# Batch 0 of a fused attention and FFN kernel: transposing raw queries, using values uncopied, and a new order of the first loads

## Chip, core and metric

The kernel runs on one core of a Trainium2 chip. The metric is device microseconds (us) of one execution, lower is better. The time before is 250.41 us, the median of three runs (249.77 to 251.29). The profile comes from a separate execution of the same program; its times count from the start of that execution's span.

## What is computed

Linear ("cosformer") attention, and a multiplicative feed-forward network on its output. There are 8 batches with 8 heads, 576 positions and 64 features a head. Inputs are fp32; the kernel works in bf16 with fp32 sums.

```python
theta = np.pi / 2.0 * pos / S                      # one angle for each position
phi(x) = concat(relu(x) * cos(theta), relu(x) * sin(theta))   # 64 -> 128 features
q_p, k_p = phi(q), phi(k)
kv  = einsum('bhsf,bhsd->bhfd', k_p, v);  z = sum(k_p, axis=2)
num = einsum('bhsf,bhfd->bhsd', q_p, kv)
den = einsum('bhsf,bhf->bhs', q_p, z) + 1e-06
x   = (num / den)  as 4608 tokens of 512
out = ((x @ w1) * (x @ w2) @ w3) @ w_out           # 512 -> 1024 -> 1024 -> 512
```

Two facts carry the change. The angle belongs to a position, so cos and sin can be multiplied in before a transpose (one number for each partition) or behind it (a row along the free dimension). And relu commutes with the transpose.

## The kernel before

**The plan.** Every instruction's place is written out by hand in the string PLAN. The loop at the end of the kernel (L801) reads it from left to right, and each entry issues its instructions on their engines' queues at once. An engine works its own queue in order; nothing is reordered. An entry `f 0; n 0 4; d 0 4` thus fixes what stands behind what on TensorE, VectorE (DVE), ScalarE (ACT), GpSimd (POOL) and on the DMA queues that POOL and SP issue to. A letter at the end of an entry (V, A, G) is the engine of a copy.

**Chunks.** A batch's 576 positions are five chunks, four of 128 and one of 64 (chunk 4). For each batch, entries load `k`, `q`, `v` (`l`, or `lg` and `lt` behind a gate; `l0` for parts of batch 0). `k b c` and `q b c` make the features of a chunk: the cos half on VectorE (L502), the sin half on ScalarE (L505). `v b c` copies the values to `va`, whose 65th column is 1, so that one matmul gives kv and z (L519). `kv b` (L548; for batch 0 `kv0`, L746) makes kv with 40 matmuls of 65 columns, and copies it to `kvs`. `qt b c` transposes a chunk's query features on TensorE, 8 transposes of 128 columns (L566), and copies them from PSUM to `qpT` (L572). `n b c` is num and den by 8 matmuls of 65 columns into the PSUM tile `pnum`, of which there is one (L580; `n0` has its own, `pfirst`). `d b c` is the division on VectorE: L589, L590, L591. `xt b c` transposes the result on TensorE (L618) and copies it into the FFN's input tile `xT` (L619); `xd b c` does this by a DMA transpose on SP's queue (L611).

**FFN.** There are nine tiles of 512 tokens. Each `f t` issues the next piece of tile t: products with w1 and w2 (L662; for the first two tiles some in quarters of 128 tokens), a copy of the first on ScalarE (L686, L700), their product `abT` on VectorE (L688, L705), and then `abT` times `w34b` (L710) and its copy out.

**The w3 stage.** w3 times w_out is made once: `w34b`. It stands in the plan between tile 0's products and the pieces that use it. `t3 jp` transposes block jp of w3 on VectorE in one instruction into one of three buffers `w3T` (L464), and `w jp lc n` multiplies it by w_out on TensorE (L480); the last is copied by ScalarE (L483).

**The start.** Keys of batch 0 are loaded through SP, everything else through POOL. TensorE runs idle matmuls on zeros (27, then 10, 3 and 3) until there is work. On POOL's queue the order of loads is: v, queries of chunks 0 and 1 (`q02`), v chunk 4, w2 columns 0 and 1, queries 2 and 3 (`q22`), the first part of batch 1's queries, query chunk 4, the second part of batch 1's queries, then the other seven pieces of w1 and w2 with w3 and w_out among and behind them, and then batch 1's keys and values.

Of the kernel before, what the change touches and what calls it, by code (L numbers as in the profile page):

```python
# [10 lines left out]
FP32 = mybir.dt.float32  # L11
BF16 = mybir.dt.bfloat16
I32 = mybir.dt.int32
ALU = mybir.AluOpType
# [21 lines left out]
f 0; xt 0 4 V  # L36
# [24 lines left out]
f 0; n 1 0; xd 1 4; d 1 0  # L61
f 0; q 2 1; v 2 4 G; lt 3 v 0; q 2 0
f 0; n 1 1; d 1 1; k 2 2
f 0; q 2 3
f 0; lg 3 q 1; v 2 1 G; l 3 v 1; q 2 4; k 2 0
f 0; n 1 2; d 1 2
f 0; xt 1 1 V; lt 3 k 0
f 1; k 2 3; xd 1 0; n 1 3; d 1 3; xt 1 2 V
f 1; qd 2 1
f 1; v 2 2 V  # L70
f 1; k 2 4; k 2 1
# [185 lines left out]
f 8  # L257
f 8
f 8; st; st; st; st; st"""
NKP, NVA, NQP, NRQ, NRV, NT3 = 1, 2, 1, 2, 2, 3  # L260


# [14 lines left out]
def _angles(nc, pool):  # L277

    s_i = pool.tile([P, 2 * NCH], I32, name="s_i")
    nc.gpsimd.iota(s_i[0:64, 0:5], pattern=[[1, 5]], base=0, channel_multiplier=5)  # L280
    nc.gpsimd.iota(s_i[64:128, 0:5], pattern=[[1, 5]], base=320, channel_multiplier=4)
    nc.gpsimd.iota(s_i[:, 5:9], pattern=[[1, 4]], base=0, channel_multiplier=4)
    nc.gpsimd.iota(s_i[:, 9:10], pattern=[[1, 1]], base=512, channel_multiplier=1)
    return s_i


def _trig_tables(nc, pool, s_i):

    th = pool.tile([P, 2 * NCH], FP32, name="th")
    nc.vector.tensor_copy(out=th[:], in_=s_i[:])  # L290
    nc.vector.tensor_scalar_mul(out=th[:], in0=th[:], scalar1=math.pi / 2 / S)
    t2 = pool.tile([P, 2 * NCH], FP32, name="t2")
    nc.vector.tensor_mul(out=t2[:], in0=th[:], in1=th[:])

    def poly(outt, coefs):
        nc.vector.tensor_scalar_mul(out=outt[:], in0=t2[:], scalar1=float(coefs[0]))
        for c in coefs[1:-1]:
            nc.vector.scalar_tensor_tensor(out=outt[:], in0=outt[:], scalar=float(c), in1=t2[:],
                                           op0=ALU.add, op1=ALU.mult)

    cosv = pool.tile([P, 2 * NCH], FP32, name="cosv")
    poly(cosv, [-1 / 3628800, 1 / 40320, -1 / 720, 1 / 24, -1 / 2, 1.0])
    nc.vector.tensor_scalar_add(out=cosv[:], in0=cosv[:], scalar1=1.0)
    sinv = pool.tile([P, 2 * NCH], FP32, name="sinv")
    poly(sinv, [-1 / 39916800, 1 / 362880, -1 / 5040, 1 / 120, -1 / 6, 1.0])
    nc.vector.scalar_tensor_tensor(out=sinv[:], in0=sinv[:], scalar=1.0, in1=th[:],
                                   op0=ALU.add, op1=ALU.mult)
    return cosv, sinv


@with_exitstack
def kernel(
# [123 lines left out]
    def clear_rows(i):  # L436

        if i < NVA:
            nc.vector.memset(va_bufs[i][:, :, :, D:D + 1], 1.0)
            nc.vector.memset(va_bufs[i][64:128, 4, :, 0:D], 0.0)  # L440
        for fp in kp_bufs[i:i + 1] + qp_bufs[i:i + 1]:
            nc.vector.memset(fp[64:128, 4, :, :], 0.0)

    clear_rows(0)
# [11 lines left out]
    cosv, sinv = _trig_tables(nc, const, _angles(nc, const))  # L456
    identb = const.tile([P, P], BF16, name="identb")
    make_identity(nc, identb[:])


    def w3_tr(jp):

        w3T = sm.tile([P, 8, 128], BF16, name="w3T", bufs=NT3)
        nc.vector.transpose(out=w3T[:].rearrange("p l (c i) -> p l c i", c=4),  # L464
                            in_=w3b[:, jp, :].rearrange("p (c l j) -> p l c j", c=4, l=8))
        w3Ts[jp] = w3T
# [95 lines left out]
    def q_tr(b, c, on):  # L562
        R = ROWS[c]
        pst = ps_tr.tile([P, 8, 128], BF16, name="pst")
        for h in range(H):
            nc.tensor.transpose(pst[:, h, :], att[b]["qp"][:, c, h, :], identb[:])  # L566
        cols = ds(columns_of(b, c), R)
        if on == "both":
            nc.scalar.copy(out=att[b]["qpT"][:, 0:4, cols], in_=pst[:, 0:4, 0:R])
            nc.vector.tensor_copy(out=att[b]["qpT"][:, 4:8, cols], in_=pst[:, 4:8, 0:R])  # L570
        else:
            on(out=att[b]["qpT"][:, :, cols], in_=pst[:, :, 0:R])  # L572

    def num(b, c, tile=None):
        rows = out_rows(b, c)
# [162 lines left out]

    def kv_first():

        kp, va = att_of(0)["kp"], att_of(0)["va"]
        att[0]["kvs"] = sm.tile([P, H, D + 1], BF16, name="kvs", bufs=2)
        halves = att[0]["halves"] = (kva[:, :], pnum()[:, 0, :])
        for c in range(NCH):
            for h in range(H):
                nc.tensor.matmul(halves[h // 4][:, ds((h % 4) * 65, 65)], lhsT=kp[:, c, h, :],  # L746
                                 rhs=va[:, c, h, 0:D + 1], start=(c == 0 and h % 4 == 0),
                                 stop=(c == NCH - 1 and h % 4 == 3))
# [34 lines left out]
    def gated_store():  # L783
# [6 lines left out]
        "f": lambda t: next(ffn[t]), "w": w34_mm, "w3": load_w3, "wo": load_wout, "w12": w12,  # L790
        "l": load, "lg": gated, "lt": behind_transposes, "l0": load_first_parts, "gx": behind_first_x,
        "k": prep_k, "q": prep_q, "v": prep_v,
        "qc": lambda b, c: prep_q(b, c, sin=False), "qs": lambda b, c, n=H: prep_q(b, c, n, cos=False),
        "kc": lambda b, c: prep_k(b, c, sin=False), "ks": lambda b, c: prep_k(b, c, cos=False),
        "qt": q_tr, "qh": q_tr_halves, "qd": q_dma, "kv": kv, "kv0": kv_first, "kvs0": kvs_first,
# [40 lines left out]
```

## Time and profile before

| what | value |
| --- | --- |
| median of three runs | 250.41 us |
| span of the profiled execution | 249.8 us |
| TensorE weight loads (PEld), busy | 129.8 us, x1855 |
| DMA share by slice, first 28 of 40 slices | 7 to 9 tenths |
| queue q0 (loads and stores by POOL), share of 16 engines | 69.9% |
| last weights of w1 and w2: issued at, us to landing | 20.41, 9.9 |
| first w1 columns: issued at, us to landing | 9.84, 10.3 |
| kv of batch 0 on TensorE | 13.53 to 14.9 |
| kv of batch 1 on TensorE | from 51.67 |

In the lines of a profile, the columns of the timeline are start, duration, engine, source line and operation, the tile written and those read, the shape, how often in a row, and in brackets how long the engine had been idle and what ended that. Matmuls are pipelined: of a group "x4 128x512" with 1.03 us, the next begins 0.86 after its start. A helper's line covers every call of it.

### The profile page before, as it was taken

Reading aid. Unit: us, or ns where it says so; the run is one execution under the profiler, and the core shown is the slowest. Engines: PE = TensorE matmul, PEld = TensorE weight load, DVE = VectorE, ACT = ScalarE, POOL = GpSimd, SP = SyncE. Lnnn points to the kernel's source line nnn. Section 1 sums busy time; section 2 is a strip of 40 time slices with the busy share of each in tenths; the row PEclk is TensorE's granted clock in tenths of the full one; section 3 lists DMA queues with packets and bytes.
Section 4 is the critical chain, followed back from the end, with each engine's and each line's share of the span. In section 5 each row is a group of like instructions: output and inputs, shape, how many; then the busy total and the mean of one; then the engine's idle time right before and its main releaser. Section 6 shows DMA issues by size and latency. Waiting matters only on the chain. (4 is left out here: it accounts for less than half of the span.)

```text
span 249.8 us, 4910 instructions
## 1 busy us (share of the span) xinstructions
PE 241.0 (96%) x1855; PEld 129.8 (52%) x1855; DVE 141.7 (57%) x342; ACT 127.1 (51%) x217; POOL 84.9 (34%) x162
## 2 busy tenths in 40 slices
PE   8978999999999999999999999899999999999994
PEld 2467754455964644445454545355444644444443
DVE  6498667958669546827684370487546506502420
ACT  2698243648567534665477324767643333323332
POOL 7764445425502043107215005307000502569200
PEclk9999999999999999999999999999999999999999
DMA  7999999999997989999999999999676561999513
GB/s 193 184 193 196 200 200 197 198 198 184 151 170 109 166 139 162 160 196 137 153 147 117 189 111 123 140 208 216 154 97 126 139 84 34 219 271 298 192 42 126
DMA packets 87223, 40.69 MB, mean 163 GB/s; under 512 B 51744, under 2 KB 84768, under 8 KB 87200
## 3 DMA queue, kind: packets, MB, share of 16 engines
q0 software_dynamic: 40144, 27.20, 69.9%
q1 hardware_dynamic: 47056, 13.18, 35.5%
q8 instruction: 14, 0.23, 0.4%
q14 instruction: 9, 0.07, 0.1%
HBM read 38.80 MB, written 9.44 MB: 193 GB/s over the span
## 5 line engine op out<-in xcount | busy, mean ns | idle before, releaser
L662 PE MATMUL ffnps<-xT,w2b 128*128 128x512 bf16 (+2 forms) x352 | 76.0, 340 | 1.7 <-ACT osb L716 1.2
L705 DVE TENSOR_TENSOR abT<-asb,ffnps 128x512 bf16<-128x512 bf16 x64 | 43.7, 684 | 59.3 <-PE ffnps L662 57.4
L662 PE MATMUL ffnps<-xT,w1b 128*128 128x512 bf16 (+2 forms) x352 | 76.0, 340 | 0.6 <-DMA xT<-xblk 0.6
L710 PE MATMUL ffnps<-w34b,abT 128*128 128x512 bf16 x280 | 64.5, 379 | 0.0
L700 ACT CAST asb<-ffnps 128x512 bf16<-128x512 f32 x64 | 37.3, 585 | 53.1 <-PE ffnps L662 43.7
L662 PEld LDWEIGHTS <-w2b 128*128 128x128 bf16 x352 | 31.5, 98 | 29.7 <-issue 1.5
L662 PEld LDWEIGHTS <-w1b 128*128 128x128 bf16 x352 | 31.6, 98 | 28.9 <-DMA xT<-xblk 1.1
L710 PEld LDWEIGHTS <-abT 128*128 128x128 bf16 x280 | 26.1, 98 | 28.3
L505 ACT ACTIVATE kp<-kf,sinv 128x512 bf16<-128x512 bf16 (+3 forms) x40 | 28.1, 720 | 9.7 <-DMA kf<-in_k_dram 9.7
L505 ACT ACTIVATE qp<-qs,sinv 128x512 bf16<-128x512 bf16 (+2 forms) x40 | 28.0, 716 | 3.1 <-DMA qs<-in_q_dram 3.1
L591 DVE TENSOR_TENSOR xblk<-pnum,den 128x512 bf16<-128x512 f32 (+1 forms) x39 | 26.9, 691 | 2.0 <-DMA xT<-xblk 0.7
L417 POOL COPY seen<-asb 128x1 bf16<-128x1 bf16 x14 | 2.7, 195 | 68.6 <-ACT asb L700 68.6
L502 DVE TENSOR_SCALAR kp<-kf,cosv 128x512 bf16<-128x512 bf16 (+3 forms) x40 | 15.9, 415 | 9.9 <-DMA kf<-in_k_dram 9.9
L580 PEld LDWEIGHTS <-qpT 128*128 128x128 bf16 x320 | 15.3, 98 | 9.8 <-issue 0.8
L716 ACT COPY early<-ffnps 128x512 f32<-128x512 f32 x19 | 11.1, 582 | 15.5 <-PE ffnps L710 15.4
L580 PE MATMUL pnum<-kvs,qpT 128*128 128x65 bf16 x312 | 16.4, 194 | 1.3 <-DVE xblk L591 0.6
L519 POOL COPY va<-vs 128x512 bf16<-128x512 bf16 (+1 forms) x17 | 10.7, 649 | 18.4 <-PE ffnps L662 9.8
L716 ACT COPY osb<-ffnps 128x512 f32<-128x512 f32 x16 | 9.4, 585 | 14.4 <-PE ffnps L710 14.4
L502 DVE TENSOR_SCALAR qp<-qs,cosv 128x512 bf16<-128x512 bf16 (+1 forms) x40 | 14.8, 389 | 0.9 <-DMA qs<-in_q_dram 0.8
L480 PE MATMUL ffnps<-early,w3T 128*128 128x512 bf16 x64 | 14.3, 379 | 0.1
L453 PE MATMUL unread<-zeros 128*128 128x512 bf16 x43 | 12.2, 451 | 1.2 <-DVE zeros L434 1.2
L650 POOL DMA_DIRECT2D out_dram<-osb x22 | 11.6, 532 | 2.9 <-DMA out_dram<-osb 2.2
(86 smaller groups left out, 187.4 us busy)
## 6 DMA issues: line engine op xcount, KB each, us to landing
out_dram<-osb POOLq DMA_DIRECT2D x10, 256.0 KB, 6.3
qs<-in_q_dram POOLq DMA_DIRECT2D x8, 256.0 KB, 8.2
early<-in_moe_w_dram POOLq DMA_DIRECT2D x8, 256.0 KB, 10.3
qs<-in_q_dram POOLq DMA_DIRECT2D x6, 320.0 KB, 8.4
kf<-in_k_dram POOLq DMA_DIRECT2D x6, 320.0 KB, 9.2
vs<-in_v_dram POOLq DMA_DIRECT2D x6, 320.0 KB, 7.6
kf<-in_k_dram POOLq DMA_DIRECT2D x6, 256.0 KB, 7.1
vs<-in_v_dram POOLq DMA_DIRECT2D x6, 256.0 KB, 8.2
```

The lines of the kernel that those rows point to most:

```text
L453: nc.tensor.matmul(unread[:, :], lhsT=zeros[:, 0:128], rhs=zeros[:], start=True, stop=True)
L480: nc.tensor.matmul(acc[:, :], lhsT=w3T[:, lc, :], rhs=woutb[:, lc, :], start=(lc == 0), stop=(lc == 7))
L502: nc.vector.tensor_scalar(out=dst[:R, c, :, 0:D], in0=src[:R, :, c, :], scalar1=0.0, scalar2=cosv[:R, at:at + 1], op0=ALU.max, op1=ALU.mult)
L505: nc.scalar.activation(out=dst[:R, c, 0:n, D:F], in_=src[:R, 0:n, c, :], func=ACTF.Relu, scale=sinv[:R, at:at + 1], bias=0.0)
L580: nc.tensor.matmul(nt[:, h // 4, ds((h % 4) * 65, 65)], lhsT=qpT[:, h, ds(at, 128)], rhs=kvs[:, h, :], start=True, stop=True)
L591: nc.vector.tensor_tensor(out=xblk[rows], in0=n4[:, :, :, 0:D], in1=den[rows].unsqueeze(3).to_broadcast([R, 2, 4, D]), op=ALU.mult)
L650: on.dma_start(out=rows[:, :, cols], in_=osb[64 * i:64 * i + rows.shape[0], :, cols])
L662: nc.tensor.matmul(out, lhsT=w[:, kc, ts(jc, 128)], rhs=x[:, kc, tok], start=(kc == 0), stop=(kc == 3))
L700: nc.scalar.copy(out=asb[:], in_=aT[:, :])
L705: nc.vector.tensor_mul(out=abT[:, jc, :], in0=asb[:], in1=bT[:, :])
L710: nc.tensor.matmul(ops[:, :], lhsT=abT[:, jc, ts(ms, 128)], rhs=w34b[:, jc, :], start=(jc == 0), stop=(jc == 7))
L716: nc.scalar.copy(out=osb[:, ms % 2, :], in_=ops[:, :])
```

## The change

In batch 0 the queries are no longer turned into features and then transposed. The raw queries of a chunk are transposed twice, into the upper and the lower 64 partitions of a PSUM tile (16 transposes of 64 rows out), and one VectorE instruction takes the maximum with 0, multiplies by a table `waves` and writes `qpT`. The table holds cos in partitions 0 to 63 and sin in 64 to 127, one column a position; it is made once by five fp32 transposes and two copies, in the memory of an output buffer. Batch 0's values are used as they were loaded: kv then takes 64 columns from the values and a 65th column from a second matmul with a column of ones, 80 matmuls in place of 40, with the chunks in the order 4, 0, 2, 3, 1. Rows 64 to 127 of chunk 4 are cleared in the raw values and queries instead of in `va` and `qp`. The transpose of a w3 block may be split in two.

The plan is rewritten from its start to the middle of tile 1 of the FFN; from the second piece of tile 1 on it is the same. Batch 1's queries are loaded behind the first half of w3 and all of w_out, and their features and transposes go into the w3 stage. Two of batch 1's chunks (4 and 0) are transposed into `xT` by TensorE and not by DMA. Of the idle matmuls 27 and 6 are left.

```diff
-l0 q02; k 0 4; k 0 0; idle 10; l0 v4; v 0 0 A; w12 1 0 2; k 0 2; l0 q22; lg 1 q 0; l0 q4; lg 1 q 1; w12 0 0 2; w12 1 4 2; w12 0 2 2; v 0 4 V; v 0 1 V; v 0 2 A; k 0 3; w12 1 6 2; idle 3; w12 1 2 2; q 0 1; w12 0 4 2; w3 3; k 0 1; w3 1; qt 0 1 V; q 0 0 4; w12 0 6 2; wo 1; qc 0 3; v 0 3 A; wo 0; kv0; q 0 2; kvs0 1 A; kvs0 0 A; w3 0; wo 3; w3 2; qh 0 0 V; wo 2; qs 0 3; n 0 1; qt 0 2 A; w3 4; d 0 1; w3 5; qt 0 3 A; q 0 4; n0; w3 6; n 0 2; d 0 0; idle 3; d 0 2; xt 0 1 V; open; w3 7; xt 0 0 A; q 1 2; q 1 0; lg 1 k 0; n 0 3; qt 0 4 V; lg 1 k 1; lg 1 v 0; lt 1 v 1; xt 0 2 A; q 1 3; q 1 1; l 2 k 0
+l0 q02; k 0 4; k 0 0; waves; idle 6; k 0 2; l0 v4; l0 q22; w12 1 0 2; l0 q4; w12 0 0 2; w12 1 2 2; w12 0 2 2; w12 1 4 2; w12 0 4 2; k 0 3; qf 0 0 8; k 0 1 4; w12 1 6 2; w12 0 6 2; w3 3; w3 1; wo 1; wo 0; qf 1 0 8; kv0; kvs0 0 A; kvs0 1 A; w3 0; wo 3; w3 2; wo 2; n0; n 0 1; d 0 0; d 0 1; qf 2 0 8; l 1 q 0; l 1 q 1; w3 4; w3 5; xt 0 0 A; n 0 2; open; xt 0 1 A; w3 6; w3 7
 f 0
-f 0; d 0 3
-f 0; l 2 v 0
-f 0; xt 0 3 V; qt 1 2 V; n 0 4; d 0 4
+f 0; qf 3 0 8; d 0 2; l 1 k 0; l 1 k 1
+f 0; n 0 3; xt 0 2 A; d 0 3; l 1 v 0; l 1 v 1
 f 0
+f 0; xt 0 3 V; qf 4 0 8; l 2 k 0
+f 0; clear 0; l 2 v 0
+f 0; n 0 4; d 0 4
 f 0; clear 1
+f 0; xt 0 4 V
...
-f 0; qt 1 0 V; lg 2 q 0; q 1 4; qt 1 3 A
-f 0; qt 1 1 V
...
-f 0; l 2 k 1; t3 0
 f 0
-f 0; t3 1; qt 1 4 A
-w 0 0 4
-w 0 4 4; l 2 q 1
-w 1 0 4
-w 1 4 4; t3 2; t3 3; t3 4
-w 2 0 4
-w 2 4 4; l 2 v 1; v 1 4 G
-w 3 0 4; v 1 3 G; t3 5; v 1 1 G
-w 3 4 4
-w 4 0 4; k 1 2; l 3 q 0; t3 6
-w 4 4 4; k 1 1; t3 7; k 1 4
-w 5 0 4
-w 5 4 4; k 1 0
-w 6 0 4; v 1 2 V
-w 6 4 4; v 1 0 V; k 1 3
-w 7 0 4; kv 1
-w 7 4 4; v 2 3 G; n 1 4; v 2 0 G
-f 0; d 1 4
-f 0; n 1 0; xd 1 4; d 1 0
+f 0; t3 0 0 4; t3 0 4 4
+w 0 0 4; t3 1; l 2 k 1
+w 0 4 4; q 1 4
+w 1 0 4; t3 2; q 1 0; l 2 q 1
+w 1 4 4
+w 2 0 4; t3 3
+w 2 4 4; qt 1 4 A; q 1 1
+w 3 0 4; l 2 v 1
+w 3 4 4; qt 1 0 V; t3 4; q 1 2; qt 1 1 A
+w 4 0 4
+w 4 4 4; t3 5; q 1 3; v 1 4 G; v 1 3 G; v 1 1 G; l 3 q 0
+w 5 0 4; qt 1 2 V; k 1 2
+w 5 4 4; t3 6; k 1 1
+w 6 0 4; k 1 4; qt 1 3 V
+w 6 4 4; t3 7; k 1 0
+w 7 0 4; v 1 2 V; k 1 3
+w 7 4 4; v 1 0 V; kv 1
+f 0; n 1 4; v 2 3 G; v 2 0 G
+f 0; d 1 4; n 1 0
...
+    oneb = const.tile([P, 1], BF16, name="oneb")
+    nc.vector.memset(oneb[:], 1.0)
+    nc.vector.memset(raw[0, "v"][64:128, :, 4, :], 0.0)
+    nc.vector.memset(raw[0, "q"][64:128, :, 4, :], 0.0)
...
+    for f in range(2):
+        nc.scalar.copy(out=spread[:, :, f, :], in_=trig[:, f, NCH:].unsqueeze(2).to_broadcast([P, NCH, D]))
+
+    def wave_rows():
+        for at, c0, n in ((0, 0, 4), (512, 4, 1)):
+            pst = ps_tr.tile([P, 512], FP32, name="pst")
+            for c in range(c0, c0 + n):
+                nc.tensor.transpose(pst[:, ts(c - c0, 128)], spread[:, c].rearrange("p f d -> p (f d)"), identf[:])
+            w = 512 if n == 4 else 64
+            nc.scalar.copy(out=waves[:, at:at + w], in_=pst[:, 0:w])
...
+    def q_tr_first(c, h0, n):
+        R = ROWS[c]
...
+        for h in range(h0, h0 + n):
+            for f in range(2):
+                nc.tensor.transpose(pst[ts(f, D), h, :], raw[0, "q"][:, h, c, :], identb[:])
+        nc.vector.scalar_tensor_tensor(out=att[0]["qpT"][:, h0:h0 + n, ds(columns_of(0, c), R)],
+                                       in0=pst[:, h0:h0 + n, 0:R], scalar=0.0,
+                                       in1=waves[:, ds(128 * c, R)].unsqueeze(1).to_broadcast([P, n, R]),
+                                       op0=ALU.max, op1=ALU.mult)
...
+        for i, c in enumerate(KV0):
             for h in range(H):
...
+                nc.tensor.matmul(out[:, 0:D], lhsT=kp[:, c, h, :], rhs=v0[:, h, c, :],
+                                 start=(i == 0 and h % 4 == 0), stop=False)
+                nc.tensor.matmul(out[:, D:D + 1], lhsT=kp[:, c, h, :], rhs=oneb[:],
+                                 start=False, stop=(i == NCH - 1 and h % 4 == 3))
```

More of the change, by code (lines that the diff above doesn't have):

```diff
@@ L69 @@
+f 0; lg 3 q 1; v 2 1 G; l 3 v 1; q 2 4; k 2 0; n 1 2; d 1 2
+f 0; xt 1 1 V; lg 3 k 0
+f 0
+f 1; k 2 3; n 1 3; d 1 3; xt 1 2 V
 f 1; qd 2 1
@@ L455, with w3_tr @@
     idle_mms(27)
-    cosv, sinv = _trig_tables(nc, const, _angles(nc, const))
+    trig = _trig_tables(nc, const, _angles(nc, const))
+    cosv, sinv = trig[:, 0, :], trig[:, 1, :]
     identb = const.tile([P, P], BF16, name="identb")
     make_identity(nc, identb[:])
[L461 to L466, printed above, removed]
+    identf = const.tile([P, P], FP32, name="identf")
+    nc.scalar.copy(out=identf[:], in_=identb[:])
+    waves = osbs[-1][:].rearrange("p i m -> p (i m)")
+    spread = osbs[-2][:].rearrange("p i m -> p (i m)")[:, 0:NCH * F].rearrange("p (c f d) -> p c f d", c=NCH, f=2)
+    for f in range(2):
[7 more added lines that the diff above has]
+            nc.scalar.copy(out=waves[:, at:at + w], in_=pst[:, 0:w])
+    def w3_tr(jp, l0=0, n=8):
+        if l0 == 0:
+            w3Ts[jp] = sm.tile([P, 8, 128], BF16, name="w3T", bufs=NT3)
+        nc.vector.transpose(out=w3Ts[jp][:, l0:l0 + n, :].rearrange("p l (c i) -> p l c i", c=4),
+                            in_=w3b[:, jp, :].rearrange("p (c l j) -> p l c j", c=4, l=8)[:, l0:l0 + n])
     def w3_dma(jp):
@@ L572, in q_tr @@
             on(out=att[b]["qpT"][:, :, cols], in_=pst[:, :, 0:R])
+    def q_tr_first(c, h0, n):
+        R = ROWS[c]
+        if h0 == 0:
+            att_of(0)["pst"] = ps_tr.tile([P, 8, 128], BF16, name="pst")
+        pst = att[0]["pst"]
+        for h in range(h0, h0 + n):
[5 more added lines that the diff above has]
+                                       op0=ALU.max, op1=ALU.mult)
     def num(b, c, tile=None):
@@ L739, in kv_first @@
     def kv_first():
-        kp, va = att_of(0)["kp"], att_of(0)["va"]
+        kp, v0 = att_of(0)["kp"], raw[0, "v"]
         att[0]["kvs"] = sm.tile([P, H, D + 1], BF16, name="kvs", bufs=2)
         halves = att[0]["halves"] = (kva[:, :], pnum()[:, 0, :])
-        for c in range(NCH):
+        for i, c in enumerate(KV0):
             for h in range(H):
-                nc.tensor.matmul(halves[h // 4][:, ds((h % 4) * 65, 65)], lhsT=kp[:, c, h, :],
-                                 rhs=va[:, c, h, 0:D + 1], start=(c == 0 and h % 4 == 0),
-                                 stop=(c == NCH - 1 and h % 4 == 3))
+                out = halves[h // 4][:, ds((h % 4) * 65, 65)]
+                nc.tensor.matmul(out[:, 0:D], lhsT=kp[:, c, h, :], rhs=v0[:, h, c, :],
+                                 start=(i == 0 and h % 4 == 0), stop=False)
+                nc.tensor.matmul(out[:, D:D + 1], lhsT=kp[:, c, h, :], rhs=oneb[:],
+                                 start=False, stop=(i == NCH - 1 and h % 4 == 3))
     def kvs_first(i, on):
```

30 lines of the change are left out of this document (14 added, 16 removed).

## The prediction

> **What bounds the kernel now.** I read the page's busy shares first, then the timeline from the start to 62 us, then the timeline around the two longest later pauses. All times are us from the start of the profiled span.
>
> ```profile
> PE 241.0 (96%) x1855; PEld 129.8 (52%) x1855; DVE 141.7 (57%) x342; ACT 127.1 (51%) x217; POOL 84.9 (34%) x162
> ...
> PE   8978999999999999999999999899999999999994
> ...
> PEclk9999999999999999999999999999999999999999
> ```
>
> TensorE is busy 96% of the span, in all slices, at the full granted clock. So from the first FFN matmul on, the kernel is one TensorE queue: whatever is added to that queue, and every pause in it, is paid in full.
>
> ```profile
> 20.80 0.39 PE L662 MATMUL ffnps<-xT,w1b 128*128 128x128 bf16 x4
> ...
> 25.01 1.05 PE L662 MATMUL ffnps<-xT,w2b 128*128 128x256 bf16 x8 [0.47 <-DMA w2b<-in_moe_w_dram]
> ...
> 38.00 0.61 PE L566 MATMUL pst<-identb,qp 128*128 128x128 bf16 x8
> 38.45 13.38 PE L480 MATMUL ffnps<-early,w3T 128*128 128x512 bf16 x60
> ...
> 45.61 5.73 PEld L480 LDWEIGHTS <-w3T 128*128 128x128 bf16 x28 [0.58 <-DVE w3T L464]
> ...
> 159.75 1.02 PE L662 MATMUL ffnps<-xT,w2b 128*128 128x512 bf16 x4 [1.22 <-ACT osb L716]
> ...
> 225.54 1.04 PE L662 MATMUL ffnps<-xT,w1b 128*128 128x512 bf16 x4 [0.60 <-DMA xT<-xblk]
> ```
>
> This is the whole budget. The FFN begins at 20.80. After it the queue pauses five times that matter: about 0.6 at 25 (weights), 0.6 at 45.6 (a transposed w3 block), 0.2 at 54, 1.4 at 159.7, 0.75 at 225.5. Everything else from 20.80 to 246.5 is work: some 222.3 us. The last 3.3 us are the last store.
>
> ```profile
> 33.00 0.69 DVE L572 COPY qpT<-pst 128x1024 bf16<-128x1024 bf16 x1 [0.55 <-PE pst L566]
> ...
> 37.15 1.24 DVE L464 STREAM_TRANSPOSE w3T<-early 128x1024 bf16<-128x1024 bf16 x1
> ...
> 38.31 0.65 DVE L705 TENSOR_TENSOR abT<-asb,ffnps 128x512 bf16<-128x512 bf16 x1
> ...
> 38.89 3.48 DVE L464 STREAM_TRANSPOSE w3T<-early 128x1024 bf16<-128x1024 bf16 x3
> ```
>
> Two things to see. A w3 block costs VectorE 1.16 to 1.24, and it now makes block 0 before the last abT and blocks 1 to 3 right behind it, so 13.38 us of w3 matmuls (L480) run with one pause of 0.58. And no copy of qpT (0.69) stands between two blocks.
>
> **The change, step by step.**
>
> *Start of the FFN.* Now the 27 idle matmuls: the pitch is 0.425 up to 6.29 and 0.214 then, so 27 end at 9.5. New are five fp32 transposes for the wave table. No fp32 matmul is in the trace; bounds are 0.06 each (a bf16 transpose, L566) and 0.32 (a 512-column matmul, 0.216, plus a weight load, 0.10): 0.3 to 1.6. I take four passes of 0.055, 1.1 in all. With six idle matmuls (1.3) that is 11.9; the first queries were issued at 3.49 and landed 7.6 later, at 11.1, so they do not decide. Two chunks of raw-query transposes are 32 x 0.058 = 1.85, to 13.75. The first kv has 80 matmuls in place of 40 that took 1.27; the 40 of one column cost between nothing and 0.032 each (the 65-column pitch, the shortest in the trace): I take 1.2, so 2.5, to 16.2. From the end of kv to the first num was 0.9 (two kvs copies, 14.85 to 15.76): 17.1. All this while VectorE has four k features, one feature multiply from PSUM, the split k chunk 1 and the second multiply, done by about 16.2, so it hides.
>
> The feature multiply (SCALAR_TENSOR_TENSOR, 1024 elements from PSUM, fp32 table) is not in the trace. The plain PSUM copy of the same size is 0.69 (L572); two 512-element PSUM products are 1.38 (L591, 0.69 each). I take one start of 0.16 and 1.04 ns an element: 1.22.
>
> VectorE runs norm 0, norm 1, then the multiply of chunk 2, and num 2 stands before the first FFN matmul. From a num to its den is 0.5 (15.76 to 16.25), a norm is 1.05: 17.1 + 0.5 + 2.1 + 1.22 = 20.9; with a semaphore 21.05. Num 2 (0.26) and the x transpose (0.22) make the FFN start at 21.55 against 20.80: **+0.75**. The copies of v (five of 0.3 to 0.6) and ten features of batch 0's queries (0.35 to 0.72) are gone, but from ACT and VectorE, which are not what is waited for here once kv itself starts at 13.75 against 13.53.
>
> *Work moved into the queue behind that start.* Num 3 (0.26) and x transpose 2 (0.22) stood ahead of it; raw queries 3 and 4 are 16 transposes each (0.92 x 2), ahead of it before and half as many; x transposes 4 and 0 of batch 1 (0.12 + 0.22) replace transposes by DMA on SP's queue, which had no one waiting at 62. The five query transposes of batch 1 stay inside (three in tile 0, now all in the w3 stage). Sum **+2.66**.
>
> *First FFN tile.* Batch 1's queries leave the POOL queue ahead of seven w1/w2 loads, 576 KB, and go behind two whole halves of w3 and w_out: at the 1.3 us per 256 KB of those rows, w1/w2 land some 3 us or more sooner and the 0.6 at 25 goes. They land about 39, before w3's second half (same bytes before it, still about 44), and are first read at 44: nothing lost. But VectorE's queue has the multiply of chunk 3 ahead of norm 2, and that multiply waits for transposes that stand behind two FFN pieces. TensorE: 0.88 of FFN, 0.92 of transposes, 0.88 of FFN, at 2.7 from the FFN's start. VectorE: multiply 2.0 to 3.2, norm 2 to 4.25. Num 3 needs both (its PSUM tile is the one norm 2 reads), so TensorE stops for 1.6. Net **+1.0**.
>
> *Into the w3 stage.* Block 0 is now made behind the last abT: 0.31 from the last FFN matmul to that abT, 0.69, a half block 0.70 (0.16 + half of 1.08), 0.06: **+1.7**, where before 38.00 ran straight into 38.45. The half split saves 0.55 of it; it cannot remove it.
>
> *Inside the w3 stage.* Query features, and three qpT copies on VectorE, stand between the blocks in its queue. Block 4 stands behind the copy of query chunk 0, which waits for its transposes, and those stand behind w3 block 3 on TensorE: copy 0.18 + 0.69, block 1.20, 0.06 = 2.13, less 0.46 (the other query transposes): a stop of 1.7. Block 6: 0.18 + 0.69 + a k feature 0.35 + 1.24 + 0.06, less half a block of matmuls 0.86: 1.65. Block 7: 2.13 less 0.86: 1.27. Together 4.6, less the 0.6 pause that is there now: **+4.0**. In bounds: none of the three has another instruction for TensorE to run, so 4.0 to 5.0.
>
> *After it.* Num 0 of batch 1 comes one FFN piece sooner behind norm 4: **+0.45**. From tile 1 on nothing changes but the clock time. The pause at 159.7 is ScalarE waiting for batch 6's keys; everything ten us later with loads not later could remove it, and perhaps that at 225.5: 0 to -2.1, I take **-1.0**.
>
> Sum: 0.75 + 2.66 + 1.0 + 1.7 + 4.0 + 0.45 - 1.0 = +9.6 on the profiled 249.8, so 259.4. The median of the three runs is 250.41, 0.6 above this execution: **260.0**.
>
> By the Trainium skill (TensorE: Matmul & The Clock Gate, "Wait — 56ns, not 53.3ns?") a warm matmul never starts less than about 25 ns after the one before, however narrow; by it the one-column matmuls would be 1.0 and not 1.2, and the estimate 259.8.
>
> **Rivals.**
>
> 1. *TensorE's clock falls before the FFN.* Between kv's end (16.2) and 21.55 TensorE has three nums or so, some transposes and one idle stretch of 2 us, and the change drops the idle matmuls that stood at 12 and 18. For: the first 12 idle matmuls ran at half pace until 6.29, 5.1 us of work. Against: the longest pause of the trace, 1.4 at 159.7, was followed by full pace. Price: half of 5.1, 2.5, less what falls into the 1.6 stop, about 2: 262. Beside it stands a rule of the Trainium skill (same page, "Part 4: PE-mode transpose" and "What's actually happening"): transposes do not count as busy, and one idle window of about 3.4 us halves the clock. By that rule this would come out; no stretch of the trace is long enough to show it.
> 2. *Regained.* The loads are a near-full resource until 175 us; if TensorE's lateness lets them get ahead, both later pauses vanish, and with the cheap ends (multiply 0.69, narrow matmuls free, fp32 transposes 0.3, which take some 3 us off start and first stop) it is 256.
> 3. *Faster: the loads decide the start.* w1 columns 0 and 1 landed at 20.1 before, just ahead of 20.80; now 832 KB behind v's last piece (11.5) they land about 16.5. If the FFN could start at 17, that is -3.8 + 2.66 - 0.6 = -1.8, with no stops: 248.6. It decides from the point where kvs is ready by 12.5; but kv needs queries' transposes from 11.1 on, 1.85 + 2.5 + 0.9. Against it also: at 21.55 + 222.3 + 2.66 + 3.3 the queue alone fills 249.8, with no stop at all.
> 4. *The change does not bring the weights sooner* (landings follow issue order loosely): the 0.6 stays: 260.6.
>
> **Chances.** Forecast (with 4) 0.64, clock 0.17, regained 0.11, faster 0.05, within 0.5% 0.03. About 0.5%, or 1.3 us, is what a measurement here tells from no change. Range: 255.5 (the regained end) to 264 (clock, no later pause regained, dear ends of the unknown costs); so faster 0.05, same 0.03, slower 0.92.
>
> **What would show it.** FFN start at 21 to 23 in the timeline; a stop of 1 to 2 before num 3; three stops of 1.3 to 1.7 in front of w3 matmuls, put down to w3T, and 1.7 at the stage's begin; the multiply at 1.1 to 1.3. It is wrong if VectorE's blocks run ahead of TensorE there, or if the FFN starts before 19.

## Result and profile after

The changed kernel takes 259.11 us, the median of four runs (258.38 to 259.59), against 250.55 for four runs of the kernel before on the same chip (249.77 to 251.29). The ratio is 1.034, with a 95% interval of 1.030 to 1.038: slower by 8.6 us. Forecast were 260.0, and 255.5 to 264.

The profiled execution of the changed kernel has a span of 257.7 (own time 259.59, the longest of the four; the spans of the four are 256.4 to 257.7). The first lines are of its page: engine totals, TensorE's busy tenths, and its granted clock, each of the 40 digits being 6.4 us.

```profile
PE 241.9 (94%) x1911; PEld 132.5 (51%) x1938; DVE 142.3 (55%) x340; ACT 123.4 (48%) x214; POOL 84.0 (33%) x161
...
PE   8869997778999999999999999999999999999994
...
PEclk9985999999999999999999999999999999999999
```

TensorE's busy time has hardly grown (241.0 to 241.9), but its share fell from 96% to 94%: the queue has new pauses, and the digits below 9 show where: up to 19 us, and from 39 to 64. The 5 in the clock row, from 19 to 26 us, was not in the row of before. Now the start, in the timeline of the changed kernel:

```profile
11.44 1.08 PE L603 MATMUL pst<-identb,qs 128*64 128x128 bf16 x32 [0.92 <-DMA qs<-in_q_dram]
12.20 1.22 DVE L604 SCALAR_TENSOR_TENSOR qpT<-pst,osb 128x1024 bf16<-128x1024 bf16 x1 [2.24 <-PE pst L603]
...
17.73 1.21 DVE L604 SCALAR_TENSOR_TENSOR qpT<-pst,osb 128x1024 bf16<-128x1024 bf16 x1
...
19.00 0.62 PE L615 MATMUL pnum<-kvs,qpT 128*128 128x65 bf16 x8 [1.77 <-DVE qpT L604]
...
19.84 0.63 PE L697 MATMUL ffnps<-xT,w1b 128*128 128x128 bf16 x4
...
25.11 0.43 PE L615 MATMUL pnum<-kvs,qpT 128*128 128x65 bf16 x8 [0.54 <-DVE xblk L626]
```

The FFN starts at 19.84, earlier than the 20.80 of before, although num 2 waits 1.77 for the third multiply (17.73 to 18.94), which stands behind two norms in VectorE's queue. But a group of four 128-column products, 0.39 in the kernel before, now lasts 0.63. The windows of the same trace (stretch, its length, busy time and instructions of PE, PEld, DVE, ACT and POOL, granted clock, DMA share, GB/s) say why:

```profile
17.00:18.00 1.00, 0.24 (x4) 0.06 (x2) 0.97 (x3) 0.58 (x1) 0.06 (x1) 0.94 1.46 192
18.00:19.00 1.00, 0.00 (x0) 0.00 (x0) 0.95 (x1) 0.00 (x0) 0.35 (x1) 0.50 1.45 196
...
23.00:24.00 1.00, 1.00 (x12) 1.00 (x11) 1.00 (x2) 0.00 (x0) 0.55 (x1) 0.50 1.46 205
24.00:25.00 1.00, 0.57 (x6) 0.30 (x3) 0.93 (x5) 0.58 (x1) 0.12 (x2) 0.65 1.45 190
```

The granted clock is 0.50 through six such windows, 0.94 in the one before them and 0.65 in the one behind. A window at 0.65 is at half pace for 0.7 of it, one at 0.94 for 0.1: about 6.8 us at half pace, from 17.9 to 24.7. Last, the w3 stage in the timeline of the changed kernel, with VectorE's copy and block ahead of the first inner stop:

```profile
40.91 5.35 PE L501 MATMUL ffnps<-early,w3T 128*128 128x512 bf16 x23 [1.47 <-DVE w3T L486]
...
48.27 1.06 PE L587 MATMUL pst<-identb,qp 128*128 128x128 bf16 x16
48.92 0.69 DVE L593 COPY qpT<-pst 128x1024 bf16<-128x1024 bf16 x1 [3.34 <-PE pst L587]
49.53 1.24 DVE L486 STREAM_TRANSPOSE w3T<-early 128x1024 bf16<-128x1024 bf16 x1
...
50.82 2.76 PE L501 MATMUL ffnps<-early,w3T 128*128 128x512 bf16 x11 [1.49 <-DVE w3T L486]
...
56.24 1.04 PE L501 MATMUL ffnps<-early,w3T 128*128 128x512 bf16 x4 [1.34 <-DVE w3T L486]
...
59.66 1.90 PE L501 MATMUL ffnps<-early,w3T 128*128 128x512 bf16 x8 [1.07 <-DVE w3T L486]
```

Four stops of TensorE, all put down to a transposed block. Before 50.82 the order can be seen in full: VectorE was idle for 3.34, because the next thing in its queue was a copy that waits for TensorE's transposes; only behind the copy comes the block, which TensorE then waits for. (The bracket counts from a group's modelled end. Counted from the start of the last matmul, as the budget below does, the stops are 1.63, 1.65, 1.51 and 1.23.)

Both profiled executions side by side. The places, before and after: first FFN matmul 20.80 and 19.84, first w3 matmul 38.45 and 40.91, end of the w3 stage and batch 1's kv 53.80 and 62.67, first product of tile 1 62.19 and 72.11, last copy 246.50 and 254.26.

| stretch of TensorE's queue | before | after | difference |
| --- | --- | --- | --- |
| start of the FFN | 20.80 | 19.84 | -0.96 |
| from there to the first w3 matmul | 17.65 | 21.07 | +3.42 |
| from there to the end of the w3 stage and batch 1's kv | 15.35 | 21.76 | +6.41 |
| from there to the first product of tile 1 | 8.39 | 9.44 | +1.05 |
| from there to the last copy | 184.31 | 182.15 | -2.16 |

In the second row five query transposes (2.3) have moved out, into the third row. The last row holds the two later pauses of before, 1.38 and 0.75: neither is in the trace after.

### The profile page after: what moved, and what is told of

Read it like the earlier page. It is cut to its first block, busy times and chain, and to the rows that moved or that the text cites. A ratio compares the mean times of both kernels' runs of the same rounds, so it can differ in the third digit from the quotient of the medians.

```text
span 257.7 us, 5031 instructions
## 1 busy us (share of the span) xinstructions
PE 241.9 (94%) x1911; PEld 132.5 (51%) x1938; DVE 142.3 (55%) x340; ACT 123.4 (48%) x214; POOL 84.0 (33%) x161
## 3 DMA queue, kind: packets, MB, share of 16 engines
HBM read 38.80 MB, written 9.44 MB: 187 GB/s over the span
## 4 chain that ended last, share of the span: by engine, by line
PE 88%; DVE 5%; DMA 3%; issue 2%; POOL 1%; ACT 0%; POOLq 0%; DVEq 0%
PE ffnps L697 48%; PE ffnps L745 23%; PE ffnps L501 5%; PE pnum L615 4%; PE pnum L569 3%; DMA qs<-in_q_dram 3%; DVE w3T L486 2%; DVE xblk L626 1%; PE pst L603 1%; DVE qpT L604 1%; PE pst L653 1%; PE pst L587 1%; PE ffnps L762 1%; PE kva L782 0%; POOL vs L393 0%
## 5 line engine op out<-in xcount | busy, mean ns | idle before, releaser
L697 PEld LDWEIGHTS <-w1b 128*128 128x128 bf16 x352 | 32.4, 100 | 28.7 <-issue 0.2
L697 PEld LDWEIGHTS <-w2b 128*128 128x128 bf16 x352 | 32.5, 100 | 28.0
L526 ACT ACTIVATE kp<-kf,trig 128x512 bf16<-128x512 bf16 (+4 forms) x40 | 27.5, 713 | 1.4 <-DMA kf<-in_k_dram 1.4
L526 ACT ACTIVATE qp<-qs,trig 128x512 bf16<-128x512 bf16 (+1 forms) x35 | 24.7, 720 | 1.6 <-DMA qs<-in_q_dram 1.6
L501 PE MATMUL ffnps<-early,w3T 128*128 128x512 bf16 x62 | 14.9, 380 | 5.5 <-DVE w3T L486 5.4
L523 DVE TENSOR_SCALAR kp<-kf,trig 128x512 bf16<-128x512 bf16 (+3 forms) x40 | 15.0, 396 | 7.0 <-DMA kf<-in_k_dram 7.0
L523 DVE TENSOR_SCALAR qp<-qs,trig 128x512 bf16<-128x512 bf16 (+1 forms) x35 | 12.4, 366 | 0.6 <-DMA qs<-in_q_dram 0.5
L501 PEld LDWEIGHTS <-w3T 128*128 128x128 bf16 x64 | 5.7, 98 | 13.0 <-DVE w3T L486 7.3
```

The costliest lines, as they stand in the source:

```text
L501: nc.tensor.matmul(acc[:, :], lhsT=w3T[:, lc, :], rhs=woutb[:, lc, :], start=(lc == 0), stop=(lc == 7))
L523: nc.vector.tensor_scalar(out=dst[:R, c, :, 0:D], in0=src[:R, :, c, :], scalar1=0.0, scalar2=cosv[:R, at:at + 1], op0=ALU.max, op1=ALU.mult)
L526: nc.scalar.activation(out=dst[:R, c, 0:n, D:F], in_=src[:R, 0:n, c, :], func=ACTF.Relu, scale=sinv[:R, at:at + 1], bias=0.0)
L697: nc.tensor.matmul(out, lhsT=w[:, kc, ts(jc, 128)], rhs=x[:, kc, tok], start=(kc == 0), stop=(kc == 3))
```

## Experiments

All versions but one (the kernel before) are made from the changed kernel, and a diff is against it where nothing else is said. Times are medians, ratios are to the kernel before in the same job, with 95% intervals. "Stop" is a pause of TensorE from the last matmul's start plus its pitch.

**Blocks ahead of the copies.** Three blocks of w3 go ahead of the copies that wait for TensorE.

```diff
-w 3 4 4; qt 1 0 V; t3 4; q 1 2; qt 1 1 A
+w 3 4 4; t3 4; qt 1 0 V; q 1 2; qt 1 1 A
...
-w 5 0 4; qt 1 2 V; k 1 2
-w 5 4 4; t3 6; k 1 1
-w 6 0 4; k 1 4; qt 1 3 V
-w 6 4 4; t3 7; k 1 0
+w 5 0 4; t3 6; qt 1 2 V; k 1 2
+w 5 4 4; k 1 1
+w 6 0 4; k 1 4; t3 7; qt 1 3 V
+w 6 4 4; k 1 0
```

> Only the order in VectorE's queue inside the w3 stage changes: w3 blocks 4, 6 and 7 stand ahead of the copies of qpT for query chunks 0, 2 and 3, not behind them. Theory (the copy waits for TensorE and the block behind it makes TensorE wait): the three stops of 1.65, 1.51 and 1.23 us shrink to some 0.4 in all, so about 4 us less: span 253.7, time near 255. Rival (VectorE simply has too much work in that stage, 17 of 20 us): the stops move to other blocks or to kv, and less than 1.5 us is won.

Measured: 255.13 (253.87 to 256.37), ratio 1.016 (1.011 to 1.021), 4.0 less than the changed kernel. In its timeline the copy is still there, and nobody waits for it:

```profile
47.74 0.69 DVE L593 COPY qpT<-pst 128x1024 bf16<-128x1024 bf16 x1 [2.00 <-PE pst L587]
...
47.99 1.89 PE L501 MATMUL ffnps<-early,w3T 128*128 128x512 bf16 x8
...
50.21 1.04 PE L501 MATMUL ffnps<-early,w3T 128*128 128x512 bf16 x4 [0.33 <-DVE w3T L486]
```

Block 4 is multiplied from 47.99 without a wait; of three stops one of 0.49 is left, before block 5. The clock did not fall in this profiled execution, so the medians could mix two things. The stage can be read by itself, at full clock in both traces: from the first w3 matmul to the end of batch 1's kv it takes 17.87 in place of 21.76, which is 3.9 less, the three stops' 4.39 less 0.49. The order of the queue on VectorE is shown to cost about 4 us.

**First block a piece earlier.** Blocks 0 and 1 are issued one piece of the FFN earlier.

```diff
-f 0
 f 0; t3 0 0 4; t3 0 4 4
-w 0 0 4; t3 1; l 2 k 1
+f 0; t3 1
+w 0 0 4; l 2 k 1
```

> Only w3 blocks 0 and 1 move: block 0 is transposed one FFN piece earlier, ahead of the last abT, and block 1 right behind it. Theory (the stop of 1.63 us at the stage's begin is abT plus half a block in VectorE's queue): it goes, 1.4 to 1.6 us less, time near 257.5, and the three later stops stay as they are. Rival (TensorE is then caught at block 2 or by the last abT's late PSUM release): under 0.7 us won.

Measured: 258.38 (257.83 to 258.82), ratio 1.028 (1.024 to 1.032), 0.7 less. The stop of 1.63 at the stage's entry is gone, but a new one of 0.50 stands before block 1 at 40.98, since that block now waits behind the last abT, and one of 0.90 at 232.56, where TensorE waits for a copy by ScalarE. A net gain of half the stop, between what the theory and the rival said: the stop is named rightly, and its price in the whole was less than its length.

**Idle matmuls kept.** Eight go in front of num 2, into its wait of 1.77.

```diff
-... xt 0 0 A; n 0 2; open; ...
+... xt 0 0 A; idle 8; n 0 2; open; ...
```

> Eight idle matmuls are added in the 1.9 us in which TensorE waits for chunk 2's query features, nothing else. Theory (the pauses and transposes before the FFN let TensorE's clock fall to half from 17.9 to 24.4 us, and the first FFN pieces run at half pace): the granted clock stays at 1.0 in the slices of 18 to 25 us, the FFN's first pieces take 0.22 for each group and not 0.43, and num 3 comes 0.8 to 1.3 us earlier: time near 258. Rival (num 3 waits for VectorE's multiply and norm anyway, so a faster clock only waits longer): the clock stays up and less than 0.4 us is won.

Measured: 257.86 (257.67 to 258.28), ratio 1.027 (1.024 to 1.030), 1.2 less. The windows of this trace, columns as above:

```profile
18.00:19.00 1.00, 1.00 (x6) 0.39 (x4) 1.00 (x2) 0.18 (x1) 0.04 (x1) 1.00 1.47 196
...
23.00:24.00 1.00, 0.20 (x7) 0.21 (x7) 0.97 (x3) 0.00 (x0) 0.37 (x1) 1.00 1.42 200
```

The clock stays at 1.00. The window from 23 to 24 shows where much of the gain went: TensorE is done sooner and waits for norm 2, a stop of 1.52 before num 3 (0.70 in the changed kernel). That is nearly the 1.6 which the prediction gave this stop at full pace.

**Norm ahead of the multiply.** In VectorE's queue norm 2 goes ahead of the multiply of chunk 3.

```diff
-f 0; qf 3 0 8; d 0 2; l 1 k 0; l 1 k 1
+f 0; d 0 2; qf 3 0 8; l 1 k 0; l 1 k 1
```

> Only norm 2 goes ahead of chunk 3's feature multiply in VectorE's queue. Theory (num 3 waits for norm 2 only because it stands behind a multiply that waits for transposes): norm 2 ends before 22 us, num 3 follows the multiply by 0.1, and the stop of 0.7 us before num 3 goes: 0.6 to 1.0 us less, time near 258.3. Rival (the chain through ScalarE's copy and abT is as long): under 0.3 us won.

Measured: 258.37 (257.97 to 259.29), ratio 1.029 (1.026 to 1.033), 0.7 less. The stop before num 3 is gone, at a mean clock of 0.985 as in the changed kernel: 0.7 is the stop's length at half pace.

**The four together.** The edits of the four versions above.

> The four edits before together: w3 blocks ahead of the copies of qpT, blocks 0 and 1 early, eight idle matmuls, norm 2 first. Alone they won 4.0, 0.7, 1.2 and 0.7 us (medians, against 259.1). Theory (each removes a stop of its own, and the clock and the norm are one chain, so that they win more together than one by one; the later pauses before tiles come back only in part): 6.6 to 7.6 us, time 251.5 to 252.5, not yet below the kernel before, because of the 1.7 to 2.7 us of added TensorE work. Rival (the kernel later waits for loads, and what is won early is lost there): the pauses near 160 and 230 us come back in full, 2.1, and the time is 253.5 or more.

Measured: 252.26 (251.26 to 253.42, ten runs), ratio 1.007 (1.003 to 1.010), 6.85 less. The single gains sum to 3.98 + 0.73 + 1.25 + 0.74 = 6.7. The FFN starts at 19.52, and the stops that are left are four of 0.48 to 0.56. So 6.85 of the 8.6 us lost are a matter of the plan that is written by hand: three changes of order, and eight idle matmuls. None of these edits undoes a part of what the change does to batch 0's queries and values.

**The loads as before.** Batch 1's queries go back ahead of w1 and w2.

```diff
-... l0 q4; w12 0 0 2; ... qf 2 0 8; l 1 q 0; l 1 q 1; w3 4; ...
+... l0 q4; l 1 q 0; l 1 q 1; w12 0 0 2; ... qf 2 0 8; w3 4; ...
```

> The changed kernel with batch 1's queries back ahead of the w1 and w2 loads on POOL's queue, the order of the kernel before. Theory (the start waits for VectorE and not for weights, so the new order of loads is worth next to nothing here): the first w1 columns land near 20, the FFN starts 0.3 to 0.6 us later, and the time is within 1 us of 259.1. Rival (the earlier weights carry a gain that the other parts hide): 2 us or more slower.

Measured: 259.23 (258.57 to 260.43), ratio 1.034 (1.027 to 1.040): not told apart from the changed kernel. The FFN starts at 19.88, and not 0.3 to 0.6 later as the theory had it, and every stop has its length. The first w1 columns (issued at 10.09, 9.7 to landing) come at 19.8, just in time. The move of these loads is worth nothing that these runs show: the FFN starts when num 2 and the x transpose behind it are done.

**Transposes by half.** The 16 raw-query transposes of a chunk first fill one half of the partitions, then the other, and do not alternate.

```diff
-        for h in range(h0, h0 + n):
-            for f in range(2):
+        for f in range(2):
+            for h in range(h0, h0 + n):
```

> The 16 transposes of a raw query chunk are issued first all into the lower 64 PSUM partitions and then all into the upper ones, in place of alternating; nothing else. They take 0.029 us each in the changed kernel, half of the 0.058 that the prediction took. Theory (two neighbours that write different halves run side by side): the pitch goes to about 0.055, chunks 0 and 1 together take 1.8 and not 0.9, the FFN starts some 0.9 us later, and chunk 4 takes 0.9 and not 0.5: time near 260.3. Rival (a weight of 64 columns is simply passed faster): pitch and time as they were.

Measured: 260.15 (258.87 to 260.6), ratio 1.036 (1.030 to 1.042). In the timeline of this run:

```profile
11.29 1.40 PE L603 MATMUL pst<-identb,qs 128*64 128x128 bf16 x32
```

32 take 1.40 in place of 1.08: less the last one's 0.16, 0.039 each against 0.029. The starts of the single transposes in the two traces say how. Alternating, two for the two halves start within 0.004 of each other, and the next two 0.056 later. Grouped, each run of eight has a pitch of 0.056, but the four runs start 0.253 apart, where one alone would take 0.45: the next run, for the other half, begins while the last three of a run have still to start. So the theory is right that transposes into different halves run side by side; it left out this overlap, and so its 1.8 for two chunks is wrong (1.2 here). The rival, which has no change, is excluded.

The time agrees with the forecast of 260.3, but not for the reason given. The FFN does not start later (19.71). In this trace 0.67 is lost between there and the w3 stage, where chunks 3 and 4 are transposed, and 0.45 behind the start of tile 1, where a pause of 0.47 stands at 120.30 that the changed kernel's trace does not have.

**An earlier start.** The edits of the first two versions, and the FFN's first two pieces ahead of num 2, so that they start as soon as x transpose 0 and the weights allow; norm 2 ahead of the multiply of chunk 3, num 3 and norm 3 a piece earlier, batch 1's num 0 a piece later, four idle matmuls.

```diff
-... n 0 1; d 0 0; d 0 1; qf 2 0 8; ... xt 0 0 A; n 0 2; open; xt 0 1 A; ...
+... n 0 1; d 0 0; d 0 1; idle 4; ... xt 0 0 A; qf 2 0 8; open; ...
-f 0
-f 0; qf 3 0 8; d 0 2; l 1 k 0; l 1 k 1
-f 0; n 0 3; xt 0 2 A; d 0 3; l 1 v 0; l 1 v 1
+f 0; xt 0 1 A
+f 0; n 0 2; d 0 2; qf 3 0 8; l 1 k 0; l 1 k 1
+f 0; l 1 v 0; l 1 v 1
...
+f 0; xt 0 2 A; n 0 3; d 0 3
...
```

> The orders of e1 and e2, and num 2 moved behind the first two FFN pieces, so that these need only x of chunk 0; norm 2 ahead of chunk 3's multiply; num 3 and norm 3 a piece earlier; four idle matmuls ahead of the first x transpose; batch 1's num 0 one FFN piece later. Theory (the FFN start was set by the program's order and not by data: weights land at 16.4, x of chunk 0 at 17.9): the FFN starts at 17.9 to 18.2 and not 19.8, no stop before num 3, clock at 1.0, time 248 to 250, below the kernel before. Rival (the second half of w3, landing near 43.5, then stops block 4 for what was won at the start): the FFN starts as early, a stop of 1 to 2 us stands before w3 block 4, and the time is 250.5 to 252.

Measured: 252.48 (251.65 to 253.08, ten runs), ratio 1.006 (1.003 to 1.009), the same as the four edits together. The timeline of this run:

```profile
17.34 0.38 PE L697 MATMUL ffnps<-xT,w1b 128*128 128x128 bf16 x4
...
43.77 1.25 DVE L486 STREAM_TRANSPOSE w3T<-early 128x1024 bf16<-128x1024 bf16 x1 [3.59 <-DMA early<-in_moe_w_dram]
...
45.07 1.25 PE L501 MATMUL ffnps<-early,w3T 128*128 128x512 bf16 x5 [1.20 <-DVE w3T L486]
```

The FFN starts 2.2 earlier than in the four edits. But TensorE reaches w3's second half before it has landed: VectorE waits 3.59 for it, and TensorE 1.36; with 0.93 before block 0, and with num 2 and x transpose 1 (0.48) now behind the start, that is 2.77, against 1.55 for the three stops that the four edits have up to the end of that stage. In the two profiled executions half of the 2.2 is left at tile 1 (63.56 against 64.68); but this one, with 251.65, is the fastest of its ten, and the medians show no gain. Where the median execution loses the rest is not shown. The rival's mechanism, that the loads of w3 decide, came true; its time, 250.5 to 252, was missed by 0.5.

**The kernel before again.** A second profile of it shows whether its later pauses return.

> The kernel before, unchanged, for a second profile. The two late pauses of its first profile (1.4 us at 159.7, waiting for batch 6's keys, and 0.75 at 225.5, waiting for a transpose by DMA) are both absent in the changed kernel. Theory (they belong to its timing, and a TensorE that is 8 us later lets the transfers get ahead): the second profile shows both, together 1.5 us or more. Rival (they belong to that one execution, whose span of 249.8 is at the slow end of 248.1 to 249.8): the second profile is shorter by about as much as the pauses shrink, and the gain that the prediction put down to lateness was mostly no gain of the change.

Measured: 250.63, span 248.7. Both pauses are there, in its timeline, but shorter:

```profile
158.93 1.02 PE L662 MATMUL ffnps<-xT,w2b 128*128 128x512 bf16 x4 [0.60 <-ACT osb L716]
...
224.50 1.04 PE L662 MATMUL ffnps<-xT,w1b 128*128 128x512 bf16 x4 [0.37 <-DMA xT<-xblk]
```

0.76 and 0.53, counted as above, against 1.38 and 0.75: together 1.29, where the theory said 1.5 or more. The places belong to the kernel, the sizes to one execution: of the 2.13 regained, 0.84 was luck of the first profile.

**w3 ahead of the queries.** The version with the earlier start, with all of w3 loaded ahead of batch 1's queries, and its blocks 0 and 1 another piece earlier; the queries' features, transposes and kv come later, the last of them between the first output pieces.

```diff
-... w3 3; w3 1; wo 1; wo 0; ... w3 0; wo 3; w3 2; wo 2; ... l 1 q 0; l 1 q 1; w3 4; ...
+... w3 3; w3 1; w3 0; w3 2; wo 1; wo 0; ... wo 3; wo 2; ... w3 6; w3 7; l 1 q 0; l 1 q 1
...
-w 7 4 4; v 1 0 V; kv 1
+w 7 4 4; qt 1 1 V; k 1 2; v 1 2 V; k 1 3
+f 0; qt 1 2 V
+f 0; qt 1 3 A; kv 1
```

> e8 with all of w3 loaded ahead of batch 1's queries (its first half ahead of w_out too), blocks 0 and 1 a piece earlier, and batch 1's query features, transposes and kv late in the w3 stage and between the first two output pieces of tile 0. Theory (in e8 the stops of 0.93 before block 0 and 1.36 before block 4 are waits for loads of w3 behind 576 KB of queries): both stops fall under 0.6, 1.3 to 1.8 us less than e8, time 250.7 to 251.2, level with the kernel before and not below it. Rival (the queries then come late and kv or num waits for their features): the stops move to kv of batch 1, and the time stays at 252 or above.

Measured: 251.63 (251.14 to 253.33, ten runs), ratio 1.005 (1.002 to 1.008): 0.85 less than the version with the earlier start, and short of the theory's 250.7 to 251.2. In the w3 stage one stop of 0.55 is left, for a load of w_out, and a new one stands in the timeline further on:

```profile
64.39 0.43 PE L615 MATMUL pnum<-kvs,qpT 128*128 128x65 bf16 x8 [1.80 <-DVE xblk L626]
```

It is the mistake of the changed kernel once more: a num waits for a norm (xblk) that stands in VectorE's queue behind features of batch 2, which nobody needed yet.

**Norm ahead of the features.** The version above, with that norm moved ahead, num 3 a piece later and two copies given to ScalarE; the diff is against that version.

```diff
-f 0; n 1 1; d 1 1; k 2 2
-f 0; q 2 3; xt 1 0 V
-f 0; lg 3 q 1; v 2 1 G; l 3 v 1; q 2 4; k 2 0; n 1 2; d 1 2; xt 1 1 V; lg 3 k 0
-f 1; k 2 3; n 1 3; d 1 3; xt 1 2 V
-f 1; qd 2 1
+f 0; n 1 1; d 1 1
+f 0; xt 1 0 A; k 2 2
+f 0; lg 3 q 1; v 2 1 G; l 3 v 1; n 1 2; d 1 2; xt 1 1 A; q 2 3; q 2 4; k 2 0; lg 3 k 0
+f 1; k 2 3
+f 1; n 1 3; d 1 3; xt 1 2 V; qd 2 1
```

> e10 with norm 2 of batch 1 ahead of batch 2's features in VectorE's queue, num 3 one FFN piece later, and two copies of x on ScalarE. Theory (the stop of 1.96 before num 3 at 64.4 in e10 is norm 2 standing behind features and copies, the same fault as norm 2 of batch 0): the stop falls to 0.4 or less and the time to 249.6 to 250.4, level with or just below the kernel before. Rival (after tile 1 the kernel follows the loads and the late features, and time won early is lost later): the stop goes and the late pauses near 160 and 225 us grow by as much; the time stays at 251 or above.

Measured: 250.92 (249.74 to 252.92, twelve runs), against 250.90 of seventeen runs of the kernel before: ratio 1.000 (0.997 to 1.0035). The stop before num 3 is gone; the time is above the theory's 249.6 to 250.4. The timeline:

```profile
17.47 0.38 PE L697 MATMUL ffnps<-xT,w1b 128*128 128x128 bf16 x4
...
35.34 9.66 PE L501 MATMUL ffnps<-early,w3T 128*128 128x512 bf16 x44 [0.50 <-DMA early<-in_moe_w_out_dram]
```

By the ratio the whole loss is back, with raw-query transposes and uncopied values as in the change. No version is shown to beat the kernel before. The FFN starts 3.33 earlier than in it, yet tile 1's first product comes at 61.79 against 62.19. Of the 3.33, 2.84 is work that now stands behind the start and not ahead of it: two chunks of raw-query transposes (0.67 each in the queue, as read below), nums 2 and 3 (0.52), x transposes 1 and 2 (0.44), batch 1's two x transposes (0.32 and 0.22). That leaves 0.1.

## Why the prediction was right, and where it was not

The size came out (260.0 against 259.11, or +9.6 against +8.6 on the median), and mostly by the mechanisms named. That it came so close is in part luck: the terms that were too high sum to 4.1, those that were too low to 2.5, and the largest of these is a clock that the sum had put at nothing.

| step | predicted | read from the two traces |
| --- | --- | --- |
| start of the FFN | +0.75 | -0.96 |
| work moved behind the start | +2.66 | +2.36 |
| first tile: stop before num 3, less the weights' pause | +1.0 | +0.1 (0.70 less 0.62) |
| clock (rival 1) | 0 | +2.2 |
| entry of the w3 stage | +1.7 | +1.63 |
| three stops inside it, less the old pause | +4.0 | +4.1 (4.39 less 0.28) |
| num 0 of batch 1 | +0.45 | +0.51 |
| later pauses | -1.0 | -2.13 |
| not accounted for | | +0.1 |
| sum on the span | +9.6 | +7.9 |

The span grew by 7.9 and the median by 8.6, since the first profile of the kernel before was of a slow execution (span 249.8; the second has 248.7). The prediction's last step took this execution for 0.6 faster than the median, but that compares a time with a span: the second profile's execution has a time of 250.63, 1.9 above its span. The forecast is the median plus 9.6 either way.

**Right, and shown.** The three stops (predicted 1.7, 1.65, 1.27, found 1.65, 1.51, 1.23), undone by reordering VectorE's queue alone, for 4.0 us. The stop at the entry (1.63) and its cause; undone, it brought 0.7 in the median. The order norm, norm, multiply ahead of num 2, and the multiply's price: 1.20 to 1.22 for a predicted 1.22. The stop before num 3: 1.6 predicted, 1.52 where the clock stayed up.

**The old pause in the w3 stage: misread.** The 0.58 at 45.61 is idle time of the weight loads (PEld), which run ahead of their matmuls. Up to batch 1's kv TensorE takes 13.22 (38.45 to 51.67) for 60 matmuls that need 12.94 at their pitch of 0.2157, so it paused for 0.28:

```profile
51.67 1.43 PE L548 MATMUL pnum<-va,kp 128*128 128x65 bf16 x40
```

The three stops thus cost 4.1 net, for a predicted 4.0. The 222.3 us of work are by the prediction's own five pauses 222.15, and 222.4 with this one put right; no term of the sum hangs on it.

**Start of the FFN: mis-sized, the chain right.** The first num was put at 17.1 and came at 15.05; from there the norms and the multiply took what was worked out. The 2.05 are: raw-query transposes 0.029 and not 0.058 each (1.02 for 32, not 1.85); the queue before them done sooner, so that the queries' landing decided, at 11.44 and not 11.9 (an fp32 transpose is 0.11 and not 0.22, and the 27 idle matmuls ended at 8.5 and not 9.5); kv 2.2, not 2.5; and 0.4 from its end to the first num, not 0.9. Against it, num 2 and the x transpose ran at half pace. Part of this is the one execution: in the profile of the first version (blocks ahead of the copies), which is the same program up to there, the idle matmuls ended at 9.96 and the first num came at 15.50. The prediction named a start between 21 and 23 as a sign, and that sign failed.

**Added work: mis-sized**, by two things. The 16 transposes of a chunk take 0.46 and not 0.92, but they take more than that from TensorE's queue:

```profile
27.35 0.39 PE L653 MATMUL pst<-identb,xblk 128*128 128x128 bf16 x4
27.67 0.64 PE L603 MATMUL pst<-identb,qs 128*64 128x128 bf16 x16
28.24 0.40 PE L697 MATMUL ffnps<-xT,w1b 128*128 128x128 bf16 x4
```

The x transposes are done with their 0.22 at 27.57, and the next products begin at 28.24: 0.67 for the chunk, with 0.1 lost on each side of it. The same 0.1 stands on each side of the 64x64 transposes of a chunk 4, in the kernel before too (30.29 to 30.61), so that batch 1's cost 0.32 and not 0.12. Why it is lost was not tested. With it the added work is 0.26 + 0.22 + 2 x 0.67 + 0.32 + 0.22 = 2.36; chunk 3, which ran at half pace, is counted at the price of full pace. Of batch 1's five query transposes all stood in tile 0 before, and not three; the sum does not depend on it.

**Clock: a rival came true inside the forecast.** Rival 1 was given 0.17, mostly because a pause of 1.4 had done nothing in the trace of before. What came ahead of the fall was not one pause, but TensorE's little work from kv's end at 14.67 to 17.9, whose longest idle piece was the last 0.8. The 2.2 in the table is what remains of the 3.42 from the FFN's start to the w3 stage, when the stops (0.70 + 1.63 less 0.62) and 1.8 of added work are taken off and the 2.3 of query transposes moved out is put back. The first version's profile, the same program up to there at full pace, agrees: that stretch takes 19.78 and not 21.07, with a stop before num 3 that is longer by 0.8. In the whole time the clock cost less, since the slower work filled these 0.8: keeping it up gave 1.2, for a rival priced at about 2.

It fell in three of the four executions (mean clock 0.985, 0.993, 0.991), and in the fourth (1.000) the span was 256.4. With the eight idle matmuls as the only edit it fell in none of four. Over all versions, the mean clock is 0.993 or less in 19 of 24 executions without idle matmuls there, in 1 of 46 with them, and in 2 of 56 of the kernel before. Where it falls, or whether, differs between executions in which TensorE has the same queue: at 17.9 in this profile, at 20.6 with the loads as before, and not at all in the first version's. The Trainium skill (TensorE: Matmul & The Clock Gate, "What's actually happening" and "Part 4: PE-mode transpose") has one idle window of about 3.4 us halve the clock, at a phase that the kernel doesn't set, and transposes not count as busy in the same way. The trace agrees on the window: 14.67 to 17.9 is 3.2, in which TensorE ran two nums and twenty transposes and nothing else, and half pace lasted 6.8, two such windows. Whether transposes count less than other matmuls no run here separates.

**Later pauses: right in kind, more than taken.** Both went, at the far end of the range given for them; the second profile of the kernel before shows that 0.84 of this belonged to one execution. In the profiles of the first two versions a pause near 230 is back (0.43 and 0.90), so its absence is not a property of the change. That TensorE's lateness is the reason was not tested.

**The loads.** Rival 4 was folded into the forecast. The pause for weights at 25 did vanish, but it is absent too with the old order of the loads. In that execution the clock was half from 20.6 to 24, which slows the pieces ahead of the weights, so whether the move would remove the pause at full pace stays open. Rival 3, that loads decide the start, is excluded for the changed kernel, whose start waits for num 2's multiply; with the start 2.2 earlier, loads of w3 did decide, as seen at 43.77.

## What to carry to other kernels

In a queue that is worked in order, an instruction that waits for another engine delays everything behind it: look in the diff for a copy or a norm placed ahead of something that the bounding engine needs soon, and price it as the wait plus what stands between. An earlier start is worth only what is not moved behind it, and less if the next loads were on time for the old one. When idle matmuls are dropped, add up TensorE's thin stretches, not its longest single pause.

## Unexpected of the hardware

Transposes of 128 positions with 64 rows out, written in turn into the two halves of the partitions, started every 0.029 us on average, in pairs within 0.004; grouped by half every 0.039; those with 128 rows out every 0.056. The Trainium skill (TensorE: Matmul & The Clock Gate, "Part 3: Packing small matmuls — row/col tiling") says of matmuls that narrow outputs at different partitions run at the same time. Both orders agree with it: the alternating one by a factor of two, the grouped one where a run for one half overlaps the run for the other. Going from 128-wide work to such transposes and back lost 0.1 each time. An fp32 transpose of 128x128 took 0.11 (five in 8.51 to 9.06), twice the bf16 one, and a matmul of kv with its weights 0.028, whether of 64 columns or of one (80 in 2.2).
